# Loads of the later batches on the SP queue, and a rearranged opening of batch 0, in a cosformer attention + SwiGLU kernel

## The chip, the cores and the metric

The kernel runs on one core of a Trainium2 chip. The metric is the time of one execution in device microseconds; where several runs are given, their median. Profiles are of one execution each, recorded by the hardware.

The engines go by the profile's names: PE (TensorE, matmuls; PEld its weight loads), DVE (VectorE), ACT (ScalarE), POOL (GpSimd), SP (SyncE). Each runs its own program in order and waits at semaphores for the others. DMAs are issued by SP and ACT (hardware queues) and by POOL (software queue, which can also convert f32 to bf16 on the way).

## What is computed

A linear attention with cosine weights on 8 batches x 8 heads x 576 positions x 64, followed by an RMS norm and a SwiGLU feed-forward layer (512 to 1536 and back) on the 4608 rows that result. Inputs and output are float32.

```python
def phi(x, c, s):
    r = np.maximum(x, 0.0)
    return np.concatenate([r * c, r * s], axis=-1)   # c, s: cos and sin of pi/2 * position / 576
q_p, k_p = phi(q, cos_w, sin_w), phi(k, cos_w, sin_w)
kv = np.einsum('bhsf,bhsd->bhfd', k_p, v);  z = np.sum(k_p, axis=2)
num = np.einsum('bhsf,bhfd->bhsd', q_p, kv)
den = np.einsum('bhsf,bhf->bhs', q_p, z)[..., None] + 1e-06
x = (num / den).transpose(0, 2, 1, 3).reshape(4608, 512)
xn = x / sqrt(mean(x * x) + 1e-6) * rms_g
g = xn @ w_gate
out = (g * sigmoid(g) * (xn @ w_val)) @ w_out
```

## The kernel before

**Tiles.** Each batch has 512 main rows, as four tiles (j = 0 to 3) of 128, and 64 rest rows; the rest rows of two batches share a tile (j = 4), and the rest rows of all batches form a ninth block of the feed-forward layer. The names, in the order of the work on a batch b:

- `raw` (six buffers): q, k or v of a batch as loaded, 1 MB; `remq`, `remk`, `remv`: the rest rows. `load_piece` and `load_rest` issue the loads on the engine that they are given.
- `q_scale`: two DVE or ACT instructions make `qp`, relu(q) times cos and times sin. `qp` has to be transposed into `qpT` (one buffer): `q_tr` does it by a DMA transpose on SP; `q_tr_pe` and `q_out`, used for batches 0 and 1, by eight PE transposes and a copy.
- `k_prep`, `v_prep`: the same scaling for k (`kp`), and v as bf16 beside a column of ones (`vv`, `vvr`).
- `kvz`: 40 small matmuls (8 heads x 5 row tiles, 65 columns) sum k'v and z into PSUM; `kvz_out` copies them to `kvzs`.
- `nd`: eight matmuls of `qpT` with `kvzs` give numerator and denominator of one row tile.
- `x_of`: on DVE `den`, `rec` (reciprocal) and `xt` (product), then on ACT the sum of squares (`scr`, `ssq`) and on POOL its power -1/2 (`rs`). `xn_scale`: one DVE instruction, `xn`. `xn` must be transposed into `xnT`: by a DMA on SP (`xn_tr`), or for batches 0 to 2 on PE (`xn_tr_pe`, and `xn_out` on ACT).
- `gval`: for each of 12 column groups nn, four matmuls into `gps` (w_gate) and four into `vps` (w_val), silu on ACT (`sil`), product on DVE (`hT`). `outp`: 48 matmuls of `hT` with `wo` into `acc`; `store` copies each quarter to `osb` on ACT and SP writes it out.

**Order.** It is written by hand. The main loop goes over blocks blk = 1 to 8 and over nn = 0 to 11; a step computes `gval(blk, nn)` and a share of `outp(blk - 1)`, and beside it the attention work that two tables (`PLAN`, in which r counts steps relative to a batch) assign to the next two or three batches. What the table lists for step r is emitted ahead of the step's matmuls or behind them, and so stands at that place in every engine's program. `loads_of` emits the loads last in a step: batch 3 in halves from r = -9 on, batches 4 to 7 in quarters from r = -16 to -5, with the rest rows of an even batch and its successor behind the last piece. They go to POOL's queue, where they stand between the `rs` instructions; SP's line holds the transposes and the stores. Batches 0 to 2 and the weights are loaded in a prologue: batch 0 on SP, everything else on POOL, which first waits, in the `gate` copy, for a piece of v.

**Opening (batch 0).** q is scaled, transposed on PE, k and v prepared; then `kvz` two heads at a time, each followed by a `kvz_out` of these two heads, and `nd`, `x_of`, `xn_scale`, `xn_tr_pe` and the first two column groups by row tile (`first_steps`), before the full 512-wide groups from nn = 2 on. PSUM has eight banks: pools `gv` (gps and vps, two buffers each: four banks), `acc` (two), `att` (one tile of two banks, for `kvz` and `nd` alike).

## Time and profile before

| | us |
|---|---|
| median of 14 runs (346.6 to 354.4) | 350.13 |
| the profiled execution | 349.61 |
| span of its instructions | 347.8 |
| PE busy, share of the span | 318.3, 91% |
| DVE, ACT, POOL busy | 195.7, 152.5, 90.7 |

A page of the profile gives the busy time of each engine, the same in 40 slices, the DMA queues, the chain of work that ended last and the costliest groups of instructions. The slices show how the run is built up: the opening lies in the first four, PE is nearly full from there on, with one dent in slice 14, and the DMA engines are busy until about two thirds of the span.

```profile
PE   1459999899899499999999999999999999999993
DVE  4754687766687498579547974793574232223300
DMA  7999997386679989868988799792022100000023
q0 software_dynamic: 12144, 29.63, 33.1%
q1 hardware_dynamic: 52304, 23.60, 32.7%
```

Each digit is the busy share of a slice in tenths; the two queues, POOL's (software) and SP's (hardware), each with packets, MB and the share of 16 DMA engines' time that they took.

### The profile page before, as it was taken

Reading aid. Unit: us, or ns where it says so; the run is one execution under the profiler, and the core shown is the slowest. Engines: PE = TensorE matmul, PEld = TensorE weight load, DVE = VectorE, ACT = ScalarE, POOL = GpSimd, SP = SyncE. Lnnn points to the kernel's source line nnn. Section 1 sums busy time; section 2 is a strip of 40 time slices with the busy share of each in tenths; the row PEclk is TensorE's granted clock in tenths of the full one; section 3 lists DMA queues with packets and bytes.
Section 4 is the critical chain, followed back from the end, with each engine's and each line's share of the span. In section 5 each row is a group of like instructions: output and inputs, shape, how many; then the busy total and the mean of one; then the engine's idle time right before and its main releaser. Section 6 shows DMA issues by size and latency. Waiting matters only on the chain.

```text
span 347.8 us, 5682 instructions
## 1 busy us (share of the span) xinstructions
PE 318.3 (91%) x2096; PEld 160.5 (46%) x2096; DVE 195.7 (56%) x423; ACT 152.5 (44%) x300; POOL 90.7 (26%) x135
## 2 busy tenths in 40 slices
PE   1459999899899499999999999999999999999993
PEld 1448555455445143544454445444544444444441
DVE  4754687766687498579547974793574232223300
ACT  4625683864554146244534453444434233223221
POOL 0618641205543154049115721310010000000000
PEclk9999999999999899999999999999999999999998
DMA  7999997386679989868988799792022100000023
GB/s 245 236 234 278 308 336 210 115 223 180 222 176 189 155 201 164 226 130 174 260 135 183 177 200 138 229 227 75 32 45 62 60 30 32 30 30 33 31 63 89
DMA packets 64476, 53.59 MB, mean 154 GB/s; under 512 B 45952, under 2 KB 53632, under 8 KB 64448
## 3 DMA queue, kind: packets, MB, share of 16 engines
q0 software_dynamic: 12144, 29.63, 33.1%
q1 hardware_dynamic: 52304, 23.60, 32.7%
q8 instruction: 16, 0.26, 0.4%
q14 instruction: 12, 0.10, 0.1%
HBM read 38.01 MB, written 9.44 MB: 136 GB/s over the span
## 4 chain that ended last, share of the span: by engine, by line
PE 74%; DMA 9%; DVE 8%; ACT 4%; issue 2%; SPq 0%; POOL 0%; ACTq 0%; DVEq 0%
PE gps L341 23%; PE vps L341 23%; PE acc L378 19%; DMA qpT<-qp 4%; PE kvz L226 3%; DVE xt L273 3%; PE nd L255 3%; DMA xnT<-xn 2%; PE acc L649 1%; DVE hT L350 1%; PE tps L197 1%; DMA raw<-in_q_dram 1%; ACT scr L281 1%; DMA remv<-in_v_dram 1%; ACT sil L349 1%
## 5 line engine op out<-in xcount | busy, mean ns | idle before, releaser
L350 DVE TENSOR_TENSOR hT<-vps,sil 128x512 bf16<-128x512 f32 x108 | 74.3, 688 | 106.7 <-PE vps L341 79.8
L341 PE MATMUL gps<-xnT,wg 128*128 128x512 bf16 (+1 forms) x456 | 113.7, 373 | 0.3 <-DMA xnT<-xn 0.2
L341 PE MATMUL vps<-xnT,wv 128*128 128x512 bf16 (+1 forms) x456 | 113.4, 372 | 0.0
L378 PE MATMUL acc<-wo,hT 128*128 128x512 bf16 x384 | 97.3, 379 | 1.0 <-DVE hT L350 1.0
L349 ACT ACTIVATE sil<-gps 128x512 bf16<-128x512 f32 x108 | 63.5, 591 | 69.4 <-PE gps L341 66.9
L341 PEld LDWEIGHTS <-wv 128*128 128x128 bf16 x456 | 44.6, 100 | 50.7 <-issue 1.1
L341 PEld LDWEIGHTS <-wg 128*128 128x128 bf16 x456 | 41.9, 100 | 41.6 <-issue 1.2
L286 POOL TENSOR_TENSOR rs<-ssq,mhalf 128x1 f32<-128x1 f32 x36 | 20.3, 564 | 152.4 <-ACT scr L281 152.4
L378 PEld LDWEIGHTS <-hT 128*128 128x128 bf16 x384 | 37.5, 98 | 46.8 <-DVE hT L350 2.0
L281 ACT ACTIVATE scr<-xt 128x513 bf16<-128x513 f32 x36 | 22.9, 636 | 69.1 <-DVE xt L273 69.1
L149 ACT COPY osb<-acc 128x512 f32<-128x512 f32 x34 | 19.9, 584 | 26.3 <-PE acc L378 24.3
L294 DVE SCALAR_TENSOR_TENSOR xn<-xt,rs,gb 128x512 bf16<-128x512 f32 x36 | 26.7, 742 | 0.8 <-POOL rs L286 0.8
L273 DVE TENSOR_TENSOR xt<-nd,rec 128x512 f32<-128x512 f32 x36 | 24.9, 692 | 1.2
L255 PE MATMUL nd<-kvzs,qpT 128*128 128x65 bf16 x256 | 14.4, 201 | 8.4 <-DMA qpT<-qp 4.8
L255 PEld LDWEIGHTS <-qpT 128*128 128x128 bf16 x256 | 12.7, 103 | 16.3 <-DMA qpT<-qp 5.3
L142 DVE TENSOR_SCALAR qp<-raw,cos_tab 128x512 bf16<-128x512 f32 x32 | 16.3, 520 | 3.7 <-DMA raw<-in_q_dram 3.7
L226 PE MATMUL kvz<-vv,kp 128*128 128x65 bf16 x256 | 12.0, 199 | 4.7 <-DVE vv L151 3.6
L98 POOL DMA_DIRECT2D raw<-in_q_dram x20 | 15.2, 763 | 2.5 <-DMA raw<-in_k_dram 2.1
L98 POOL DMA_DIRECT2D raw<-in_k_dram x20 | 15.5, 779 | 1.2 <-DMA wg<-in_moe_w_gate_dram 0.8
L142 DVE TENSOR_SCALAR kp<-raw,cos_tab 128x512 bf16<-128x512 f32 x32 | 15.5, 492 | 0.0
L98 POOL DMA_DIRECT2D raw<-in_v_dram x20 | 15.4, 772 | 0.0
L226 PEld LDWEIGHTS <-kp 128*128 128x128 bf16 x320 | 11.9, 101 | 6.9 <-ACT kp L140 2.0
(65 smaller groups left out, 192.3 us busy)
## 6 DMA issues: line engine op xcount, KB each, us to landing
out_dram<-osb SPq DMA_DIRECT2D x32, 256.0 KB, 3.0
raw<-in_q_dram POOLq DMA_DIRECT2D x16, 256.0 KB, 6.5
raw<-in_k_dram POOLq DMA_DIRECT2D x16, 256.0 KB, 8.5
raw<-in_v_dram POOLq DMA_DIRECT2D x16, 256.0 KB, 3.6
raw<-in_q_dram POOLq DMA_DIRECT2D x2, 1024.0 KB, 12.6
raw<-in_k_dram POOLq DMA_DIRECT2D x2, 1024.0 KB, 13.6
raw<-in_v_dram POOLq DMA_DIRECT2D x2, 1024.0 KB, 10.5
wg<-in_moe_w_gate_dram POOLq DMA_DIRECT2D x3, 512.0 KB, 6.4
```

The lines of the kernel that those rows point to most:

```text
L98: eng.dma_start(out=raws[what, b][:, h0 : h0 + n, :], in_=src[b, h0 : h0 + n, 0:SM, :].rearrange("h (p j) d -> p h (j d)", j=NJ),)
L142: nc.vector.tensor_scalar(out=dst, in0=src, scalar1=tab[lanes, col : col + 1], scalar2=0.0, op0=ALU.mult, op1=ALU.max,)
L226: nc.tensor.matmul(kvz_ps[b][:, h // 2 % 2, c0 : c0 + DE], lhsT=kp[:, c, h, :], rhs=vv[:, c, h, :] if c < NJ else vvr[:, b % 2, h, :], sta ...
L255: nc.tensor.matmul(ps[rows, h // HH, (h % HH) * DE : (h % HH + 1) * DE], lhsT=src[:, h, cols], rhs=kz[:, h, :], start=True, stop=True,)
L273: nc.vector.tensor_tensor(out=xt[:, 0:DM].rearrange("p (g h d) -> p g h d", g=2, d=D), in0=ndv[:, :, :, 0:D], in1=rec[:, :].rearrange("p ( ...
L281: nc.scalar.activation(out=scr[:, :], in_=xt[:, :], func=AF.Square, scale=DM**-0.5, accum_out=ssq[:, :],)
L286: nc.gpsimd.tensor_tensor(out=rs[:, :], in0=ssq[:, :], in1=mhalf[:, :], op=ALU.pow)
L294: nc.vector.scalar_tensor_tensor(out=t[:, :], in0=xt[:, 0:DM], scalar=rs[:, 0:1], in1=gb[:, :], op0=ALU.mult, op1=ALU.mult,)
L341: nc.tensor.matmul(ps[:, c0 : c0 + n], lhsT=w[:, dt, nn * P : (nn + 1) * P], rhs=xnTs[blk][:, dt, c0 : c0 + n], start=(dt == 0), stop=(dt ...
L349: nc.scalar.activation(out=sil[:, :], in_=gps[:, :], func=AF.Silu)
L350: nc.vector.tensor_tensor(out=hTs[blk][:, nn, :], in0=vps[:, :], in1=sil[:, :], op=ALU.mult)
L378: nc.tensor.matmul(acc[:, :], lhsT=hTs[blk][:, nn, j * P : (j + 1) * P], rhs=wo[:, nn, :], start=(nn == 0), stop=(nn == NNT - 1),)
```

## The change

Parts:

1. `loads_of` (batches 3 to 7) issues on SP instead of POOL.
2. Every second piece of batch 0's q, and the second half of its k, are issued by ACT instead of SP.
3. POOL's `gate` waits for the second half of k instead of a piece of v; the first 512 columns of w_gate and w_val are loaded as two times 256.
4. Opening: `kvz` of batch 0 in one go into a tile of a new pool `nd` (two tiles of two banks, on the banks that `gv` takes afterwards), one `kvz_out` on DVE, and `nd` tiles in `nd` and `att`; `x_of` of three row tiles ahead of the first `xn_scale`.
5. `keep_warm`: matmuls of `ident` with a tile of zeros whose result nobody reads, at seven places of the opening.
6. `kvzs` is laid out by PSUM bank, so that `kvz_out` is one copy of 520 columns; it goes to ACT in batches 1 to 7, where before ACT and DVE each copied a half.

DVE's order in the opening, from the last casts of v on. Before:

```order
L151 CAST vv<-raw 128x4x2x64 x2
L151 CAST kvzs<-kvz 128x130 x2
L265 TENSOR_SCALAR den<-nd 128x8
L270 RECIPROCAL rec<-den 128x8
L273 TENSOR_TENSOR xt_100<-nd,rec 128x512
L265 TENSOR_SCALAR den<-nd 128x8
L270 RECIPROCAL rec<-den 128x8
L273 TENSOR_TENSOR xt_101<-nd,rec 128x512
L294 SCALAR_TENSOR_TENSOR xn<-xt_100,rs,gb 128x512
L265 TENSOR_SCALAR den<-nd 128x8
L270 RECIPROCAL rec<-den 128x8
L273 TENSOR_TENSOR xt_102<-nd,rec 128x512
```

And after the change, from the second row tile's xt on:

```order
L276 TENSOR_TENSOR xt_101<-nd,rec 128x512
L268 TENSOR_SCALAR den<-nd 128x8
L273 RECIPROCAL rec<-den 128x8
L276 TENSOR_TENSOR xt_102<-nd,rec 128x512
L297 SCALAR_TENSOR_TENSOR xn<-xt_100,rs,gb 128x512
L268 TENSOR_SCALAR den<-nd 128x8
L273 RECIPROCAL rec<-den 128x8
L276 TENSOR_TENSOR xt_103<-nd,rec 128x512
L297 SCALAR_TENSOR_TENSOR xn<-xt_101,rs,gb 128x512
L297 SCALAR_TENSOR_TENSOR xn<-xt_102,rs,gb 128x512
L297 SCALAR_TENSOR_TENSOR xn<-xt_103,rs,gb 128x512
```

The third xt has moved ahead of the first xn, and two xn now stand between the fourth xt and its own xn, where before there was one.

SP's line around batch 3's q transposes (in the program from block 1, step 2, to block 2, step 6; qpT is a transpose of q, qprT one of rest rows, xnT_108 the transposed rest rows, out_dram a store). Before:

```order
L187 DMA_TRANSPOSE qpT<-qp 128x8x128 x5
L363 DMA out_dram<-osb 128x512
L211 DMA_TRANSPOSE qprT<-qpr 128x8x128
L187 DMA_TRANSPOSE qpT<-qp 128x8x128
L309 DMA_TRANSPOSE xnT_108<-xn 128x4x128
L187 DMA_TRANSPOSE qpT<-qp 128x8x128
L363 DMA out_dram<-osb 128x512
L187 DMA_TRANSPOSE qpT<-qp 128x8x128
```

After the change, first up to the store:

```order
L188 DMA_TRANSPOSE qpT<-qp 128x8x128 x4
L99 DMA raw<-in_q_dram 128x4x256 x2
L99 DMA raw<-in_k_dram 128x4x256 x2
L99 DMA raw<-in_v_dram 128x4x256 x2
L99 DMA raw<-in_q_dram 128x2x256 x4
L111 DMA remq<-in_q_dram 64x8x64 x2
L188 DMA_TRANSPOSE qpT<-qp 128x8x128
L366 DMA out_dram<-osb 128x512
```

Then on from the store:

```order
L99 DMA raw<-in_k_dram 128x2x256
L212 DMA_TRANSPOSE qprT<-qpr 128x8x128
L188 DMA_TRANSPOSE qpT<-qp 128x8x128
L99 DMA raw<-in_k_dram 128x2x256
L312 DMA_TRANSPOSE xnT_108<-xn 128x4x128
L188 DMA_TRANSPOSE qpT<-qp 128x8x128
L366 DMA out_dram<-osb 128x512
L99 DMA raw<-in_k_dram 128x2x256
L188 DMA_TRANSPOSE qpT<-qp 128x8x128
```

All of batch 3 and the q of batch 4 (12 loads) now stand between batch 2's last transpose and batch 3's first, and one quarter of batch 4's k before each further transpose of batch 3.

The diff:

```diff
...
     iota_f = consts.tile([P, 1], FP32, name="iota_f")
     gate = consts.tile([P, 1], FP32, name="gate")
     mhalf = consts.tile([P, 1], FP32, name="mhalf")
+    zeros = consts.tile([P, SM], BF16, name="zeros")
     warm = consts.tile([P, 1], FP32, name="warm")
     raws = {}
...
     kvzs = {}
     kvz_ps = {}
-    def kvz(b, h0, n):
+    def slot_of(h):
+        return h // 2 % 2, h // HH * 2 + h % 2
+    def kvz(b, h0, n, pool="att"):
         if h0 == 0:
-            kvz_ps[b] = pools["att"].tile([P, 2, 512], FP32, name="kvz", tag="att")
-            kvzs[b] = kvz_pool.tile([P, H, DE], BF16, name="kvzs", tag="kvzs")
+            kvz_ps[b] = pools[pool].tile([P, 2, 512], FP32, name="kvz", tag=pool)
+            kvzs[b] = kvz_pool.tile([P, 2, HH, DE], BF16, name="kvzs", tag="kvzs")
         for h in range(h0, h0 + n):
-            c0 = (h // HH * 2 + h % 2) * DE
+            c0 = slot_of(h)[1] * DE
             for c in range(NJ + 1):
                 nc.tensor.matmul(
-                    kvz_ps[b][:, h // 2 % 2, c0 : c0 + DE], lhsT=kp[:, c, h, :],
+                    kvz_ps[b][:, slot_of(h)[0], c0 : c0 + DE], lhsT=kp[:, c, h, :],
                     rhs=vv[:, c, h, :] if c < NJ else vvr[:, b % 2, h, :],
                     start=(c == 0), stop=(c == NJ),
                 )
-    def kvz_out(b, bank, eng, pairs=slice(0, 2)):
-        dst = kvzs[b][:, :, :].rearrange("p (a g i) e -> p g a i e", g=2, i=2)
-        src = kvz_ps[b][:, bank, 0 : HH * DE].rearrange("p (a i e) -> p a i e", a=2, i=2)
-        copy(eng, dst[:, bank, pairs, :, :], src[:, pairs, :, :])
+    def kvz_out(b, eng):
+        src = kvz_ps[b][:, :, 0 : HH * DE].rearrange("p g (h e) -> p g h e", e=DE)
+        copy(eng, kvzs[b][:, :, :, :], src)
     nds = {}
     xts = {}
     x_count = []
     xnTs = {}
-    def nd(b, j):
-        ps = pools["att"].tile([P, 2, 512], FP32, name="nd", tag="att")
+    def nd(b, j, pool="att"):
+        ps = pools[pool].tile([P, 2, 512], FP32, name="nd", tag=pool)
         parts = (
             [(slice(0, P), qpT, slice(j * P, (j + 1) * P), kvzs[b])]
             if j < NJ
...
             for h in range(H):
                 nc.tensor.matmul(
                     ps[rows, h // HH, (h % HH) * DE : (h % HH + 1) * DE],
-                    lhsT=src[:, h, cols], rhs=kz[:, h, :], start=True, stop=True,
+                    lhsT=src[:, h, cols], rhs=kz[:, slot_of(h)[0], slot_of(h)[1], :], start=True, stop=True,
                 )
         nds[b, j] = ps
...
     for e in range(4):
-        load_piece("q", q, 0, 2 * e, 2, nc.sync)
+        load_piece("q", q, 0, 2 * e, 2, nc.scalar if e % 2 else nc.sync)
     for e in range(2):
-        load_piece("k", k, 0, HH * e, HH, nc.sync)
+        load_piece("k", k, 0, HH * e, HH, nc.scalar if e % 2 else nc.sync)
     for what, src in (("k", k), ("v", v)):
         load_rest(what, src, 0, nc.sync)
     for e in range(4):
...
     )
     nc.gpsimd.iota(iota_i[:, :], pattern=[[0, 1]], base=0, channel_multiplier=1)
     masks.make_identity(nc, ident[:, :])
-    nc.gpsimd.tensor_copy(out=gate[:, :], in_=raws["v", 0][:, 2, 0:1])
-    load_wgv(0)
+    nc.gpsimd.tensor_copy(out=gate[:, :], in_=raws["k", 0][:, HH, 0:1])
+    load_wgv(0, 256)
+    load_wgv(256, 256)
     load_wgv(512)
     load_first("q", 1)
     load_first("k", 1)
+    nc.vector.memset(zeros[:, :], 0.0)
     nc.vector.memset(warm[:, :], 0.0)
     nc.vector.memset(mhalf[:, :], -0.5)
     for t in xt_ring:
...
-    for name, bufs in (("gv", 2), ("acc", 2), ("att", 1)):
-        pools[name] = ctx.enter_context(
-            tc.tile_pool(name="ps" + name, bufs=bufs, space=bass.MemoryType.PSUM)
-        )
+    def open_psum(name, bufs):
+        return tc.tile_pool(name="ps" + name, bufs=bufs, space=bass.MemoryType.PSUM)
     V, A = nc.vector, nc.scalar
-    q_scale(0, 0, V, A)
-    q_scale(0, 1, V, A)
-    q_scale(0, 2, V, A)
-    q_tr_pe(0, 0)
-    q_out(0, 0, V)
-    q_scale(0, 3, V, A)
-    for j, eng in ((1, A), (2, V), (3, A)):
-        q_tr_pe(0, j)
-        q_out(0, j, eng)
-    for c in range(NJ):
-        k_prep(0, c, V, A if c < 3 else V)
-    k_prep(0, NJ, V, V)
-    v_prep(0, NJ, V)
-    for e in range(4):
-        v_prep_heads(0, 2 * e, 2, A if e % 2 else V)
-    for e in range(4):
-        kvz(0, 2 * e, 2)
-        kvz_out(0, e % 2, V if e % 2 else A, slice(e // 2, e // 2 + 1))
+    for name, bufs in (("acc", 2), ("att", 1)):
+        pools[name] = ctx.enter_context(open_psum(name, bufs))
+    def keep_warm(n, pool="fill"):
+        ps = pools[pool].tile([P, SM], FP32, name="fill", tag=pool)
+        for _ in range(n):
+            nc.tensor.matmul(ps[:, :], lhsT=ident[:, :], rhs=zeros[:, :], start=True, stop=True)
+    with open_psum("fill", 1) as pools["fill"]:
+        keep_warm(12)
+        q_scale(0, 0, V, A)
+        q_scale(0, 1, V, A)
+        q_scale(0, 2, V, A)
+        q_tr_pe(0, 0)
+        q_out(0, 0, V)
+        q_scale(0, 3, V, A)
+        for j, eng in ((1, A), (2, V), (3, A)):
+            keep_warm(2)
+            q_tr_pe(0, j)
+            q_out(0, j, eng)
+        keep_warm(8)
+        for c in range(NJ):
+            k_prep(0, c, V, A if c < 3 else V)
+        k_prep(0, NJ, V, V)
+        v_prep(0, NJ, V)
+        for e in range(4):
+            v_prep_heads(0, 2 * e, 2, A if e % 2 else V)
+    with open_psum("nd", 2) as pools["nd"]:
+        kvz(0, 0, H, "nd")
+        kvz_out(0, V)
+        keep_warm(2, "acc")
+        nd(0, 0, "nd")
+        nd(0, 1)
+        nd(0, 2, "nd")
+        x_of(0, 0)
+        x_of(0, 1)
+        nd(0, 3)
+        x_of(0, 2)
+        keep_warm(8, "acc")
+    pools["gv"] = ctx.enter_context(open_psum("gv", 2))
     def first_steps(j):
         for nn in range(2):
             gval_mm(0, nn, j * P, P)
-    nd(0, 0)
-    x_of(0, 0)
-    nd(0, 1)
-    x_of(0, 1)
-    nd(0, 2)
     xn_scale(0, 0)
-    x_of(0, 2)
     xn_tr_pe(0, 0)
     xn_out(0, 0)
-    nd(0, 3)
+    x_of(0, 3)
     xn_scale(0, 1)
+    first_steps(0)
     xn_tr_pe(0, 1)
     xn_out(0, 1)
-    first_steps(0)
-    x_of(0, 3)
-    xn_scale(0, 2)
-    xn_tr_pe(0, 2)
-    xn_out(0, 2)
-    first_steps(1)
-    xn_scale(0, 3)
-    xn_tr_pe(0, 3)
-    xn_out(0, 3)
-    first_steps(2)
+    for j in (2, 3):
+        xn_scale(0, j)
+        xn_tr_pe(0, j)
+        xn_out(0, j)
+        first_steps(j - 1)
     first_steps(3)
     gval_end(0, 0)
     gval_end(0, 1)
...
         i, e = divmod(r - first, cut)
         what, src = (("q", q), ("k", k), ("v", v))[i]
         n = H // cut
-        load_piece(what, src, b, n * e, n, nc.gpsimd)
+        load_piece(what, src, b, n * e, n, nc.sync)
         if e == cut - 1 and b % 2 == 0:
-            load_rest(what, src, b, nc.gpsimd)
-            load_rest(what, src, b + 1, nc.gpsimd)
+            load_rest(what, src, b, nc.sync)
+            load_rest(what, src, b + 1, nc.sync)
     def plan_of(**whats):
         plan = {}
...
             elif what == "v":
                 v_prep(b, n, V if b == 2 and n % 2 else A)
             elif what == "kvz_out":
-                kvz_out(b, 0, A)
-                kvz_out(b, 1, V)
+                kvz_out(b, A)
             elif what == "xn_out":
                 xn_out(b, n)
             elif what == "x":
...
         accs[0, j] = pools["gv"].tile([P, DM], FP32, name="acc", tag="gv"[j % 2])
     for nn in range(NNT):
         if nn == 0:
-            kvz_out(1, 0, A)
-            kvz_out(1, 1, V)
+            kvz_out(1, A)
         if nn in (1, 3, 5, 7):
             x_of(1, nn // 2)
         if nn in (4, 6, 8, 10):
```

## The prediction

> **What bounds the kernel now.** I read the page first, then busy time by stretches, then what TensorE (PE) waits for, then the timeline of the two stretches that lose time.
>
> ```profile
> span 347.8 us, 5682 instructions
> PE 318.3 (91%) x2096; PEld 160.5 (46%) x2096; DVE 195.7 (56%) x423; ACT 152.5 (44%) x300; POOL 90.7 (26%) x135
> ```
>
> PE is busy 91% of the span, so a gain can only come from its idle time, or from time in which it is busy but slow. The stretches show where those are (start:end, length, busy time of PE, PEld, VectorE (DVE), ScalarE (ACT), GpSimd (POOL), granted clock, DMA share, GB/s).
>
> ```profile
> 0.00:32.70 32.70, 16.50 (x185) 14.46 (x186) 17.21 (x62) 15.68 (x31) 12.86 (x24) 1.00 0.99 251
> 32.70:114.80 82.10, 79.92 (x595) 40.80 (x594) 59.16 (x123) 48.35 (x95) 31.55 (x44) 1.00 0.83 215
> 114.80:123.10 8.30, 3.48 (x16) 1.57 (x17) 3.27 (x8) 1.93 (x6) 2.04 (x4) 0.79 1.03 153
> 123.10:137.30 14.20, 13.57 (x82) 6.17 (x81) 13.62 (x30) 7.65 (x16) 8.09 (x12) 1.00 1.07 175
> 137.30:331.40 194.10, 193.73 (x1170) 92.68 (x1171) 101.74 (x202) 75.94 (x150) 36.14 (x53) 1.00 0.52 117
> 331.40:347.80 16.40, 11.06 (x52) 4.80 (x49) 0.69 (x1) 2.93 (x5) 0.00 (x0) 0.90 0.32 80
> ```
>
> From 137.3 to 331.4 PE misses 0.4 us of 194: nothing can be won there, only lost. The tail after 331.4 isn't touched. What is left is the opening, with 16.2 us of idle PE, and one hole at 114.8, with 4.8 us of it and a granted clock of 0.79. The list of what PE waits for names the same places.
>
> ```profile
> PE nd L255 <- DMA qpT<-qp: 4.8, 1, 4.8
> ...
> PE nd L255 <- DVE xt L273: 3.4, 5, 1.2
> ```
>
> **The opening, step by step.** Its timeline, with the rows that carry the steps (start, length, engine, line, operation; in brackets the idle time before it and what ended it):
>
> ```profile
> 0.74 2.00 SPq L98 DMA_DIRECT2D raw<-in_q_dram  x4
> 6.97 1.28 DVE L142 TENSOR_SCALAR qp<-raw,cos_tab 128x512 bf16<-128x512 f32 x3 [3.68 <-DMA raw<-in_q_dram]
> 11.99 0.18 POOL L400 COPY gate<-raw 128x1 f32<-128x1 f32 x1 [10.51 <-DMA raw<-in_v_dram]
> 15.29 0.38 PE L226 MATMUL kvz<-vv,kp 128*128 128x65 bf16 x4 [3.56 <-DVE vv L151]
> ...
> 19.40 0.29 DVE L151 CAST kvzs<-kvz 128x130 bf16<-128x130 f32 x1 [1.93 <-PE kvz L226]
> 19.75 0.60 PE L255 MATMUL nd<-kvzs,qpT 128*128 128x65 bf16 x8 [0.45 <-DVE kvzs L151]
> 20.38 0.17 DVE L265 TENSOR_SCALAR den<-nd 128x8 f32<-128x8 f32 x1 [0.69 <-PE nd L255]
> 20.82 0.69 DVE L273 TENSOR_TENSOR xt<-nd,rec 128x512 f32<-128x512 f32 x1
> ...
> 26.36 0.69 DVE L273 TENSOR_TENSOR xt<-nd,rec 128x512 f32<-128x512 f32 x1
> 28.53 0.75 DVE L294 SCALAR_TENSOR_TENSOR xn<-xt,rs,gb 128x512 bf16<-128x512 f32 x1 [0.82 <-POOL rs L286]
> ...
> 29.48 0.63 PE L341 MATMUL gps<-xnT,wg 128*128 128x128 bf16 x4
> ...
> 31.16 0.39 PE L341 MATMUL gps<-xnT,wg 128*128 128x128 bf16 x4
> ...
> 31.61 0.39 PE L341 MATMUL gps<-xnT,wg 128*128 128x128 bf16 x4
> ...
> 32.68 1.02 PE L341 MATMUL gps<-xnT,wg 128*128 128x512 bf16 x4
> ```
>
> The same four matmuls take 0.63 us at 29.48 and 0.39 us at 31.16: before about 30 us PE runs at a slower pace, though the clock column says 1.00 (the rows decide). Two rows from later give the prices of a warm PE and of a wider copy:
>
> ```profile
> 51.89 1.25 PE kvz L226 x40
> ```
>
> ```profile
> 108.00 0.43 DVE L151 CAST kvzs<-kvz 128x260 bf16<-128x260 f32 x1
> ```
>
> *Loads to kvz (6.97 to 15.29).* Four q issues on SP take 2.00 us, 0.5 each; with every second one on ACT's queue the last leaves 1 us earlier. The transfers themselves aren't shortened, so I take half of it, 0.5 us. [...] Bounds: 1 us lost to 1.3 us won. Term: **-0.5**.
>
> *kvz to the first nd (15.29 to 19.75, 4.46 us).* Four rounds of ten matmuls, each waiting for a copy of the round before out of the one PSUM tile, become 40 matmuls and one copy. At the warm price that is 1.25; the copy costs 0.43 for 260 columns and 0.29 for 130, so about 0.14 for 130 more and 0.71 for 520; 0.35 goes for the two hand-overs. 2.3 instead of 4.46: **-2.15**. With PE at its slow pace (four rounds of about 0.7, 2.8 in all) it would be -0.6.
>
> *The x chain (20.38 to 29.28, 8.9 us).* nd now has three tiles in flight, so DVE never waits for PE: den, rec, xt take 1.13 us (20.38 to 21.51). In the new order (see the rows of DVE in the change) the fourth xt ends after four of these and one xn of 0.7, at 5.2 us, where before it was at 26.36 + 0.69 - 20.38 = 6.7. The last xn then starts 1.48 us after it, as before (27.05 to 28.53: ACT's square, POOL's power), because the two xn between them take as long. 5.2 + 1.5 + 0.75 = 7.45: **-1.45**; another -0.15 because a warm nd gives its first result sooner (0.63 from 19.75 to 20.38 before).
>
> *Last xn to the first full group (29.28 to 32.68, 3.4 us).* PE was behind by then at its slow pace. Warm, what remains is a transpose, two first_steps of 0.9 each (two pairs of gps and vps, 0.45 from 31.16 to 31.61) and 0.4 for the rest, 2.2: **-1.2**.
>
> The dummy matmuls (12, 2, 2, 2, 8, 2, 8 of them) fill time in which PE waits anyway: at 0.22 us each warm, the longest batch is 1.7 us, and the last of these lies beside 4 us of DVE work. They cost nothing if PE arrives before its inputs; if one is late by a whole batch, 1.7.
>
> Opening: **-5.4**; with each term at its bound -1.2 to -6.7 (the best of the x chain leaves out the 0.3 that POOL's power is now awaited). What could take it back is the weights, since PE then asks for everything 5.4 us sooner:
>
> ```profile
> 44.63 0.78 POOL L131 DMA_DIRECT2D wo<-in_moe_w_out_dram  x1 [0.77 <-DMA wo<-in_moe_w_out_dram]
> ```
>
> ```profile
> DMA to landing us min/median/max: 11.3/11.3/11.3
> ```
>
> ```profile
> 61.17 1.89 PE L649 MATMUL acc<-wo,hT 128*128 128x512 bf16 x8
> ```
>
> This last third of wo lands at 55.9; its first use is the second half of the row at 61.17, at 62.0, or 56.6 after the change. The queue ahead of it starts earlier, too: the gate row waited until 11.99 for a piece of v, and k's second half is issued four issues of 0.5 to 1 us ahead of that piece. So it just holds; if the queue doesn't start earlier, up to 1 us is lost, which stays inside the bounds.
>
> **The hole at 114.8.**
>
> ```profile
> 119.62 0.62 PE L255 MATMUL nd<-kvzs,qpT 128*128 128x65 bf16 x8 [4.85 <-DMA qpT<-qp]
> 120.05 1.90 PE L341 MATMUL gps<-xnT,wg 128*128 128x512 bf16 x4
> 121.73 1.56 PE L341 MATMUL vps<-xnT,wv 128*128 128x512 bf16 x4
> ...
> 124.04 1.02 PE L341 MATMUL gps<-xnT,wg 128*128 128x512 bf16 x4
> ```
>
> PE waits 4.85 us for the third transpose of batch 3's q, and then runs two groups slowly: 1.90 - 1.02 and 1.56 - 1.02 are 1.4 us more. Together 6.3. Why the transpose was late, from the chain, from SP's and from POOL's timeline:
>
> ```profile
> 105.70 13.87 DMA qpT<-qp
> ```
>
> ```profile
> 73.45 23.49 SPq L187 DMA_TRANSPOSE qpT<-qp  x5
> ...
> 105.70 3.73 SPq L187 DMA_TRANSPOSE qpT<-qp  x1
> ```
>
> ```profile
> 102.07 2.19 POOL L98 DMA_DIRECT2D raw<-in_k_dram  x3
> ```
>
> Issued 9 us ahead of its use, it took 13.87 us to land, and SP itself was held 3.73 us, while three k quarters and what follows on POOL's queue ran on the same DMA engines: the stretch 114.8 to 123.1 has them at 1.03 busy with only 153 GB/s. After the change those loads stand in SP's line, one between two transposes (see SP's rows). By the order, batch 3 and the q of batch 4 go out in one burst of 12 loads behind batch 2's four transposes and ahead of batch 3's first. Of the five transposes from 73.45 on these are four and one: the four end by about 79, the fifth at 96.94, 18 us apart; 4.3 MB at the 251 GB/s of the opening are 17 us, so the burst is just over when the fifth is due. From there the third transpose has two transposes, one xnT and two quarter loads of 256 KB (1 us each) ahead of it: it lands some 5 us after issue instead of 14.
>
> Not all 6.3 come back, because **DVE is late next**: in 114.8 to 137.3 it works 3.27 + 13.62 = 16.9 of 22.5 us, so no more than 5.6 can go, and I leave it 0.4 of small waits. Term: **-5.2**, bounds 0 to -6.3.
>
> SP's own time: 12 loads and three remainders more in a block are about 8 us of issue in 32 us (194.1 / 6), beside ten transposes of 1.3 and five stores. It fits. The loads wait for no busy buffer: each reuses a tile whose readers finished over ten steps before. The one wider kvzs copy on ACT in blocks 1 to 7 hides behind the 2 us between kvz and nd: nothing.
>
> **Sum.** The profiled execution took 349.61, its span 347.8 and 1.8 around it. -5.4 - 5.2 gives 339.0; the median of the 14 runs, 350.13, lies 0.5 higher, so I predict 339.5.
>
> **The rivals.**
>
> *The transposes stay late.* For it: the engines are the same 16, and they were full. Against it: they moved only 153 GB/s then, so the mix, not the sum, was slow. Only the opening counts: 344.7. [...]
>
> *PE stays slow in the opening,* because DVE-bound gaps of up to 2 us lie between the dummy batches. Then kvz gives -0.6 and the first_steps give nothing: -2.7 instead of -5.4, 342.2. For it: the group at 29.48 is still slow, although by then PE has worked with short breaks for ten us. [...]
>
> *Slower: SP's line becomes the bound.* Each transpose now waits for the loads before it, in every block.
>
> ```profile
> L309 SPq DMA_TRANSPOSE xnT<-xn x1: 1191/1191/1191, 159.2 to 159.2; - x1
> ...
> DMA to landing us min/median/max: 7.7/7.7/7.7
> ```
>
> ```profile
> 170.63 1.03 PE L341 MATMUL gps<-xnT,wg 128*128 128x512 bf16 x4
> ```
>
> The last xnT that block 4 needs at 170.6 lands at 166.9: 3.7 us to spare. If it lands more than that later, PE stalls, and pays 1.4 more for the slow groups behind it. In the five blocks 4 to 8, stalls of 0.7 + 1.4 already eat the gain, so it decides at landings of about 12 us; the 13.87 above shows that such exist. With 1.5 us stalls: 339.5 + 5 x 2.9 = 354. Against it: those long landings are with two queues competing.
>
> **Chances.** Forecast 0.60, transposes stay late 0.18, PE stays slow 0.14, SP bound 0.08. The forecast's own range is 337 to 342 (both terms at their best give 337.1); taking in the first two rivals and 0.5 of scatter, 336.5 to 346. The SP rival is left out with its 0.08. A measurement of this kernel tells about 0.5% (1.8 us) from no change: faster 0.92, within 0.03, slower 0.05.
>
> **What would show it.** In the new profile: kvz at about 14.8 with no copy inside its 40 matmuls, the first nd near 17, the first 512-wide group near 27; 128-wide groups of four at 0.39 us from the start; no wait of nd for qpT; qpT landing under 8 us; DVE nearly without a break where the hole was, and perhaps a wait of PE for hT at the end of block 2. Wrong would be: a first 512-wide group after 30, nd or gps waiting for a transpose in any block from 3 on, or weights that end a wait between 27 and 60.

## The result, and the profile after

The changed kernel takes 339.17 us (median of 10 runs, 337.95 to 341.39) against 349.63 us for the kernel before on the same chips (median of 47 runs, 346.60 to 354.40 but for one of 565.93): a ratio of 0.9717, 95% interval [0.9693, 0.9742], or 2.8% less time. The execution that was profiled took 338.81 us. Its page, with the slices of PE and the two queues that the change shifts bytes between:

```profile
PE 320.5 (95%) x2132; PEld 158.4 (47%) x2132; DVE 190.5 (57%) x416; ACT 152.9 (45%) x298; POOL 42.5 (13%) x71
...
PE   7669999999899999999999999999999999999994
...
q1 hardware_dynamic: 73792, 39.86, 46.0%
q0 software_dynamic: 7920, 12.32, 14.7%
```

The dent in slice 14 is gone, the opening is fuller (part of that is dummy work: PE's busy time rose by 2.2 us), and 16 to 17 MB have moved from q0 to q1. The busy time by stretches (columns as in the prediction; the cuts are the first full group, the first group of block 3, and the same 194.1 us from there as before):

```profile
0.00:28.50 28.50, 20.78 (x220) 12.99 (x221) 17.56 (x62) 14.70 (x29) 14.00 (x26) 0.94 1.08 276
28.50:127.20 98.70, 95.09 (x693) 48.01 (x693) 72.94 (x156) 58.30 (x115) 18.61 (x28) 1.00 0.83 219
127.20:321.30 194.10, 193.69 (x1172) 92.56 (x1171) 99.29 (x199) 76.95 (x150) 9.91 (x18) 1.00 0.47 118
```

The opening is 4.2 us shorter (32.7 to 28.5), the stretch from there to block 3 is 5.9 us shorter (before 82.1 + 8.3 + 14.2 = 104.6), the long stretch is as full as it was (193.69 of 194.10), and the tail behind it gives the last 0.7 (16.4 to 15.7). In the list of what PE waits for, no wait of nd for qpT is left. In its place stand the waits that come next: nd for xt, and the output matmuls for hT. Both are seen in PE's timeline of block 2:

```profile
110.18 0.41 PE L258 MATMUL nd<-kvzs,qpT 128*128 128x65 bf16 x8
...
116.10 0.57 PE L258 MATMUL nd<-kvzs,qprT 128*64 128x65 bf16 x16 [0.52 <-DVE xt L276]
...
126.96 0.39 PE L381 MATMUL acc<-wo,hT 128*128 128x512 bf16 x1 [0.90 <-DVE hT L353]
```

The third nd, at 110.18, starts without a bracket: its transpose was there. 0.52 and 0.90 us are handed back to DVE. The two q transposes issued between 100 and 110 us landed this many us after their issue:

```profile
DMA to landing us min/median/max: 2.8/3.4/3.9
```

### The profile page after: what moved, and what is told of

Read it like the earlier page. It is cut to its first block, busy times and chain, and to the rows that moved or that the text cites. A ratio compares the mean times of both kernels' runs of the same rounds, so it can differ in the third digit from the quotient of the medians.

```text
span 337.0 us, 5731 instructions
## 1 busy us (share of the span) xinstructions
PE 320.5 (95%) x2132; PEld 158.4 (47%) x2132; DVE 190.5 (57%) x416; ACT 152.9 (45%) x298; POOL 42.5 (13%) x71
## 3 DMA queue, kind: packets, MB, share of 16 engines
q1 hardware_dynamic: 73792, 39.86, 46.0%
q0 software_dynamic: 7920, 12.32, 14.7%
q10 hardware_dynamic: 1072, 1.05, 0.9%
## 4 chain that ended last, share of the span: by engine, by line
PE 80%; DVE 12%; ACT 4%; issue 3%; DVEq 0%; ACTq 0%
PE gps L344 24%; PE vps L344 24%; PE acc L381 21%; DVE hT L353 3%; PE kvz L230 3%; DVE xt L276 3%; PE fill L463 3%; DVE xn L297 2%; PE nd L258 2%; PE acc L664 2%; ACT sil L352 1%; ACT scr L284 1%; PE tps L198 1%; DVE rec L273 1%; DVE qp L143 1%
## 5 line engine op out<-in xcount | busy, mean ns | idle before, releaser
L344 PE MATMUL gps<-xnT,wg 128*128 128x512 bf16 (+1 forms) x456 | 111.9, 368 | 1.2 <-ACT xnT L150 1.1
L344 PE MATMUL vps<-xnT,wv 128*128 128x512 bf16 (+1 forms) x456 | 111.9, 368 | 0.0
L381 PE MATMUL acc<-wo,hT 128*128 128x512 bf16 x384 | 97.3, 379 | 1.5 <-DVE hT L353 1.5
L297 DVE SCALAR_TENSOR_TENSOR xn<-xt,rs,gb 128x512 bf16<-128x512 f32 x36 | 26.7, 743 | 2.0 <-POOL rs L289 2.0
L150 ACT CAST vv<-raw 128x512 bf16<-128x512 f32 x26 | 14.8, 620 | 4.0 <-DMA raw<-in_v_dram 4.0
L143 DVE TENSOR_SCALAR qp<-raw,cos_tab 128x512 bf16<-128x512 f32 x32 | 15.0, 478 | 2.4 <-DMA raw<-in_q_dram 2.4
L258 PEld LDWEIGHTS <-qpT 128*128 128x128 bf16 x256 | 11.5, 97 | 9.8 <-issue 2.4
L143 DVE TENSOR_SCALAR kp<-raw,cos_tab 128x512 bf16<-128x512 f32 x32 | 15.3, 485 | 0.0
L258 PE MATMUL nd<-kvzs,qpT 128*128 128x65 bf16 x256 | 12.9, 193 | 2.2 <-DVE xt L276 1.8
L463 PE MATMUL fill<-zeros,ident 128*128 128x512 bf16 x36 | 12.0, 481 | 2.3 <-DVE warm L411 2.3
L230 PE MATMUL kvz<-vv,kp 128*128 128x65 bf16 x256 | 10.8, 193 | 2.2 <-ACT vv L150 2.2
L230 PEld LDWEIGHTS <-kp 128*128 128x128 bf16 x320 | 10.7, 97 | 4.3 <-ACT vv L150 2.7
L664 PE MATMUL acc<-wo,hT 128*128 128x512 bf16 x48 | 11.5, 379 | 0.0
```

What stands on the lines that cost most here:

```text
L143: nc.vector.tensor_scalar(out=dst, in0=src, scalar1=tab[lanes, col : col + 1], scalar2=0.0, op0=ALU.mult, op1=ALU.max,)
L150: nc.scalar.copy(out=dst, in_=src)
L230: nc.tensor.matmul(kvz_ps[b][:, slot_of(h)[0], c0 : c0 + DE], lhsT=kp[:, c, h, :], rhs=vv[:, c, h, :] if c < NJ else vvr[:, b % 2, h, :], ...
L258: nc.tensor.matmul(ps[rows, h // HH, (h % HH) * DE : (h % HH + 1) * DE], lhsT=src[:, h, cols], rhs=kz[:, slot_of(h)[0], slot_of(h)[1], :], ...
L297: nc.vector.scalar_tensor_tensor(out=t[:, :], in0=xt[:, 0:DM], scalar=rs[:, 0:1], in1=gb[:, :], op0=ALU.mult, op1=ALU.mult,)
L344: nc.tensor.matmul(ps[:, c0 : c0 + n], lhsT=w[:, dt, nn * P : (nn + 1) * P], rhs=xnTs[blk][:, dt, c0 : c0 + n], start=(dt == 0), stop=(dt ...
```

## The experiments

The kernels compute all of the reference. "Block 2" is the time from ACT's first silu of block 2 to the first of block 3, "full group" the start of the first 512-wide group; both come from the profiled execution, the medians from all runs. Each ratio is to the kernel before as it ran beside that kernel, so ratios compare better than medians from different rows; two rows whose intervals overlap are not told apart.

| kernel | median us (range) | ratio to before, 95% | full group | block 2 |
|---|---|---|---|---|
| before | 349.63 (346.60 to 354.40, one 565.93) | 1 | 32.68 | 40.78 |
| the change | 339.17 (337.95 to 341.39) | 0.9717 [0.9693, 0.9742] | 28.51 | 35.06 |
| queue alone | 343.38 (342.68 to 343.75) | 0.9823 [0.9769, 0.9877] | 31.93 | 35.08 |
| opening alone | 344.53 (341.94 to 345.35) | 0.9839 [0.9780, 0.9899] | 27.28 | 41.95 |
| last 8 dummies removed | 340.06 (339.01 to 340.62) | 0.9721 [0.9673, 0.9768] | 29.67 | 35.07 |
| dummies moved | 337.87 (337.56 to 339.17) | 0.9669 [0.9621, 0.9717] | 27.23 | 35.06 |
| loads on ACT | 339.94 (338.39 to 340.67) | 0.9735 [0.9695, 0.9775] | 28.67 | 35.95 |
| no dummies | 340.08 (339.64 to 340.89) | 0.9741 [0.9703, 0.9778] | 30.60 | 35.06 |
| batch 0 on one queue | 340.09 (339.85 to 340.64) | 0.9747 [0.9715, 0.9779] | 29.40 | 35.05 |
| the change again | 339.15 (337.90 to 339.47) | 0.9696 [0.9669, 0.9723] | 27.31 | 35.07 |
| dummies moved, again | 337.88 (337.09 to 339.20) | 0.9668 [0.9640, 0.9697] | 27.74 | 35.07 |
| loads on ACT, bunched | 345.00 (343.53 to 347.00) | 0.9871 [0.9802, 0.9940] | 27.55 | 40.08 |
| loads on POOL, paced | 338.78 (338.30 to 339.66) | 0.9677 [0.9634, 0.9721] | 27.09 | 36.11 |
| dummies moved, 8 more | 337.89 (337.24 to 340.04) | 0.9645 [0.9619, 0.9670] | 29.75 | 35.07 |

### The two halves apart

The queue alone, in the kernel before (and the same lines back to `nc.gpsimd` in the changed kernel, for the opening alone):

```diff
-        load_piece(what, src, b, n * e, n, nc.gpsimd)
+        load_piece(what, src, b, n * e, n, nc.sync)
...
-            load_rest(what, src, b, nc.gpsimd)
-            load_rest(what, src, b + 1, nc.gpsimd)
+            load_rest(what, src, b, nc.sync)
+            load_rest(what, src, b + 1, nc.sync)
```

> The kernel before, with only the loads of batches 3 to 7 moved to SP's line. Theory (the transposes were late because loads on the second, software queue competed with them): the wait of nd for qpT at 114.8 (4.85 us) and the 1.4 us of slow groups behind it go, a wait for hT of about 1 us comes at the end of block 2, qpT lands under 5 us; block 3 starts 5.7 us earlier, 349.6 - 5.7 = 344. Rival (the hole went because the opening moved everything): the wait stays at 4 to 5 us, time 349 to 350.

> The changed kernel with the loads of batches 3 to 7 back on POOL's queue. Theory: the opening keeps its 4.2 to 4.4 us (first 512-wide group at 28.5, block 2 at 92.1), and a wait of nd for qpT of 4 to 5 us is there again in block 2, with a qpT that takes over 10 us to land: 349.6 - 4.4 = 345.2. Rival (the hole depends on the timing of the opening): no such wait, 339 to 340.

Both came out within a us of the forecast: 343.38 and 344.53. Against the 349.08 of the kernel before in the runs beside them the queue gives 5.7 and the opening 4.55 us, 10.25 together, and the whole change gave 10.5 (the ratios multiply to 0.967, measured 0.9717, which the two intervals allow): no sign that one half depends on the other. With the queue alone PE has no wait for qpT, and the three q transposes issued between 100 and 112 us land in 2.9 to 4.6 us. With the opening alone the hole is there as before. PE's row, and the landing of the two q transposes issued between 100 and 110 us in that run:

```profile
114.94 0.62 PE L258 MATMUL nd<-kvzs,qpT 128*128 128x65 bf16 x8 [5.41 <-DMA qpT<-qp]
```

```profile
DMA to landing us min/median/max: 11.3/13.1/14.8
```

Block 2 takes 40.78 and 41.95 us with the loads on POOL and 35.08 and 35.06 with them on SP, behind the old and the new opening. The queue alone keeps the two half copies of `kvzs`, so the one wide copy of part 6 gives nothing in block 2. The parts of the opening (3 and 4) were not tried one by one; their shares are read from the steps of the profile further down.

### Why the transposes were late: which queue, or how many loads at once

With the loads on POOL the same run shows what stood beside the late transposes (SP's and POOL's timeline):

```profile
95.79 0.69 POOL L289 TENSOR_TENSOR rs<-ssq,mhalf 128x1 f32<-128x1 f32 x1 [4.76 <-ACT scr L284]
96.43 2.19 POOL L99 DMA_DIRECT2D raw<-in_k_dram  x3
98.61 1.62 POOL L111 DMA_DIRECT2D remk<-in_k_dram  x2
...
100.06 4.92 SPq L188 DMA_TRANSPOSE qpT<-qp  x1
100.23 0.70 POOL L99 DMA_DIRECT2D raw<-in_v_dram  x1
...
106.12 4.81 SPq L188 DMA_TRANSPOSE qpT<-qp  x1
```

POOL had waited for ACT's square until 95.79 (its `rs`), and then issued six loads in 4.5 us: three of k, two rests of k, and at 100.23 one of v (six, where two of the expectations below speak of eight). So the change did two things: it put the loads on another queue, and it spaced them, since on SP they stand between transposes that wait for their inputs. Three kernels take these apart. First, ACT's hardware queue (q10 on that run's page, where SP's is q1), which isn't in line with the transposes but is paced by ACT's work in each step (`nc.sync` becomes `nc.scalar` in the three lines above):

> The changed kernel, with the loads from batch 3 on issued by ScalarE (a hardware queue of their own, one or two loads per step of the block) in place of SP. Theory 'software queue, issued in bunches': the transposes were late because GpSimd, held by its own waits, issued eight loads within 4.5 us beside them through the software queue; ScalarE issues its loads one per step, so the time from the first silu of block 2 to that of block 3 stays near 35.1 us, transposes land in under 6 us, and the run takes 338.5 to 341 us (72 issues lie in ScalarE's idle time). Rival 'only one line helps': the transposes are late whenever loads go through any other queue, because only the order within one queue keeps loads away from them; then block 2 takes 40 to 42 us and the run 344 to 346 us.

339.94 us and 35.95 for block 2: the rival falls, the loads needn't be in the transposes' line. One number of the theory was off, a landing of 7.0 us where under 6 was expected. PE did not wait for it, as the transposes are issued some 9 us ahead of their use (at 101.31 and 103.99, for nd at 110.68 and 113.76). Then the two ways to separate the queue from the spacing: six loads on ACT's queue issued one behind the other, and POOL's software queue held to the pace of the steps.

```diff
-                if b < B:
+                if b < B and not (b == 4 and -11 <= r <= -8):
                     loads_of(b, r)
+                if b == 4 and r == -10:
+                    for late in range(-11, -7):
+                        loads_of(b, late)
```

> As the run with ScalarE's queue, but six of batch 4's loads (three pieces of k, both rests of k, the first piece of v) are issued one behind the other in the third step of block 2, about as GpSimd did beside the late transposes. Theory 'bunch': so many loads at once beside the transposes make them late, whatever the queue; then transposes land 10 us or more after their issue there, block 2 takes 38 to 42 us and the run 342 to 346 us. Rival 'software queue': its loads alone make the transposes late, one hardware queue beside another does not; then the landings stay under 8 us, block 2 at 35.9 to 36.5 us, and the run at 339.5 to 340.5 us.

```diff
-    def loads_of(b, r):
+    def loads_of(b, r, pace):
...
-        load_piece(what, src, b, n * e, n, nc.sync)
+        nc.gpsimd.tensor_copy(out=gate[:, :], in_=pace)
+        load_piece(what, src, b, n * e, n, nc.gpsimd)
...
-                    loads_of(b, r)
+                    loads_of(b, r, hTs[blk][:, nn, 0:1])
```

> The changed kernel, with the loads from batch 3 on issued by GpSimd through the software queue again, but each held back by a small copy (128x1, into a tile that nothing reads) that reads the hT of the step in which it is issued, so that the loads go out one or two per step and not eight in 4.5 us. Theory 'bunch': then the transposes land within 7 us, block 2 takes 35 to 36.5 us and the run 338.8 to 340.5 us. Rival 'software queue': a transpose beside a load of that queue is late also when there is only one; then landings of 8 us and more stay, block 2 takes 38 us or more and the run 342 to 346 us.

The bunch on ACT cost 5 us, as its theory had it, but not by its mechanism. The three q transposes issued between 97 and 110 us landed in

```profile
DMA to landing us min/median/max: 4.4/4.5/5.0
```

so they weren't late. What was late is ACT itself. Its issues (ACTq) and its silu, and below them the same two rests where ACT issues one or two loads per step:

```profile
102.01 3.94 ACTq L111 DMA_DIRECT2D remk<-in_k_dram  x2
...
107.06 0.60 ACT L352 ACTIVATE sil<-gps 128x512 bf16<-128x512 f32 x1 [6.67 <-DMA qpT<-qp]
...
108.20 0.41 PE L258 MATMUL nd<-kvzs,qpT 128*128 128x65 bf16 x8 [3.55 <-ACT kvzs L150]
```

```profile
103.28 1.31 ACTq L111 DMA_DIRECT2D remk<-in_k_dram  x2
```

Two rest loads took 3.94 us to issue, where 1.31 was enough when the loads came step by step. The silu stands behind these issues in ACT's program and started when they were done: ACT had computed nothing for 6.67 us (the bracket names a transpose, but the last issue, of 0.37 us at 106.59, ends just ahead of the silu), and PE waited 3.55 us for the kvzs copy behind it. The issues themselves were stretched and so lay apart; it isn't a clean bunch on the DMA engines, and whether one would have made the transposes late on a hardware queue stays open.

The paced software queue is the clear one: 338.78 us, no slower than the change, with the loads on the queue that was suspected. Its timeline at the place, and the landings of the two q transposes of 101.02 and 103.00:

```profile
101.02 1.26 SPq L188 DMA_TRANSPOSE qpT<-qp  x1
...
101.65 0.73 POOL L99 DMA_DIRECT2D raw<-in_k_dram  x1 [0.16 <-issue]
...
103.00 1.49 SPq L188 DMA_TRANSPOSE qpT<-qp  x1
103.04 0.73 POOL L99 DMA_DIRECT2D raw<-in_k_dram  x1 [0.28 <-issue]
103.77 1.38 POOL L111 DMA_DIRECT2D remk<-in_k_dram  x2
...
105.27 0.71 POOL L99 DMA_DIRECT2D raw<-in_v_dram  x1
...
113.91 0.42 PE L258 MATMUL nd<-kvzs,qpT 128*128 128x65 bf16 x8 [2.06 <-DMA qpT<-qp]
```

```profile
DMA to landing us min/median/max: 3.9/7.4/10.9
```

The transpose with one load in the 2 us behind its issue landed in 3.9 us, the one with four in the 2.3 us behind it in 10.9, and only for that one in the whole run did PE wait, 2.06 us; block 2 took 1.05 us longer than in the change (36.11 against 35.06). Both theories had a number wrong: landings within 7 us didn't hold, and block 2 didn't take 38. What the runs show is that spacing the loads on the software queue takes nearly all of the loss away. It doesn't take the rests of k for it: in the kernel before, a transpose issued at 130.44 us, with three q loads issued from 129.90 on and three of k from 132.09 on, landed in 10.0 us. How many loads make a transpose late isn't settled: in the paced run one issued at 184.60 us, with three loads in the 2.3 us behind it, landed in 2.8.

### The opening: dummy matmuls and PE's pace

In the profile of the changed kernel the opening gained less than its steps had promised. PE, DVE, ACT and POOL from the first nd on:

```profile
16.10 0.91 PE L258 MATMUL nd<-kvzs,qpT 128*128 128x65 bf16 x24 [0.36 <-DVE kvzs L152]
...
18.77 0.42 PE L258 MATMUL nd<-kvzs,qpT 128*128 128x65 bf16 x8 [1.76 <-DVE xt L276]
19.03 3.36 PE L463 MATMUL fill<-zeros,ident 128*128 128x512 bf16 x8
22.18 0.63 PE L318 MATMUL tpx<-ident,xn 128*128 128x128 bf16 x4
22.85 0.59 ACT L150 COPY xnT<-tpx 128x512 bf16<-128x512 bf16 x1 [2.29 <-PE tpx L318]
23.33 0.64 ACT L284 ACTIVATE scr<-xt 128x513 bf16<-128x513 f32 x1
24.13 0.55 POOL L289 TENSOR_TENSOR rs<-ssq,mhalf 128x1 f32<-128x1 f32 x1 [2.94 <-ACT scr L284]
24.72 0.75 DVE L297 SCALAR_TENSOR_TENSOR xn<-xt,rs,gb 128x512 bf16<-128x512 f32 x1 [1.95 <-POOL rs L289]
```

Read it from the end: the last xn waits 1.95 us for POOL, POOL for ACT's fourth square, which stands behind the first xnT copy in ACT's line; that copy waits for the first tpx, and tpx for eight dummy matmuls that take 3.36 us, 0.43 each, although its xn was ready at 20.40 (19.66 + 0.74). The clock granted to PE shows the same: 0.50 from 19.4 to 22.7 us, where a second profile of the same kernel (shown below) has 1.00 throughout (columns as in the stretches; the clock is the third number from the end):

```profile
19.40:22.70 3.30, 3.30 (x12) 1.38 (x10) 3.23 (x7) 0.85 (x4) 1.10 (x2) 0.50 1.24 206
19.40:22.70 3.30, 2.57 (x27) 1.56 (x26) 3.19 (x8) 2.38 (x7) 1.24 (x3) 1.00 1.25 206
```

The half pace follows a gap of 1.76 us; the eight nd right behind the gap still run at full pace (0.42 us, 0.62 when slow). Two kernels, one without the last eight dummies, one with eight of them moved into that gap and four left behind it:

```diff
         nd(0, 2, "nd")
+        keep_warm(8, "acc")
         x_of(0, 0)
...
-        keep_warm(8, "acc")
+        keep_warm(4, "acc")
```

> The changed kernel without its last eight dummy matmuls. In the changed kernel these take 3.36 us (0.43 each) because PE had gone slow in the 1.76 us gap before them, and the first transpose of xn starts at 22.18, 1.8 us after its xn. Theory: without them that transpose starts at about 20.5 and the last xn ends near 24.0 instead of 25.5, but PE does the 128-wide groups at the slow pace (0.63 us for four instead of 0.39), so the first 512-wide group comes at 27.5 to 28.8 and the time is 338.3 to 339.5. Rival (the dummy matmuls keep nothing fast): the 128-wide groups stay at 0.39, first 512-wide group at 26.8, 337.4.

> The changed kernel with eight dummy matmuls between the third and the fourth nd of the opening, where PE idles for 1.76 us, and four instead of eight behind the fourth nd. Theory (the gap makes PE slow): all twelve take 0.22 us each, the first transpose of xn starts at 20.4 instead of 22.2, the last xn ends near 23.8, first 512-wide group at 26.7 instead of 28.5, time 337.4. Rival (PE is slow there for the low share of work before, not for this gap): they take 0.43 each, the fourth nd comes 1.7 us later than before, the first 512-wide group at 28.5 to 30, time 339 to 341.

Without the last eight, the gap of 1.76 is followed by one of 1.27, and PE's groups are slow far into the first column groups:

```profile
19.55 0.42 PE L258 MATMUL nd<-kvzs,qpT 128*128 128x65 bf16 x8 [1.76 <-DVE xt L276]
21.25 0.61 PE L318 MATMUL tpx<-ident,xn 128*128 128x128 bf16 x4 [1.27 <-DVE xn L297]
...
22.91 0.63 PE L344 MATMUL vps<-xnT,wv 128*128 128x128 bf16 x4
```

340.06 us: worse than either theory had it (up to 339.5). In its profile kvz, too, started 0.78 us later than in the first profile of the change (14.72 against 13.94). By the medians the eight are worth 0.9 us, but the ratios, 0.9721 and 0.9717, don't tell the two kernels apart. With the gap filled the groups take 0.39 us from the first on:

```profile
17.73 1.67 PE L463 MATMUL fill<-zeros,ident 128*128 128x512 bf16 x7
...
22.42 0.39 PE L344 MATMUL vps<-xnT,wv 128*128 128x128 bf16 x4
```

The full group then starts at 27.23, and the run takes 337.87 us (26.7 and 337.4 were expected, but kvz started 0.67 us later than in the profile that these come from). But the opening alone, whose program is that of the changed kernel up to batch 3's loads, had shown its eight dummies at full pace behind the same gap. So both were run again, side by side:

> The changed kernel once more, beside the version with four of its dummy matmuls moved. In two profiled executions with the same opening the eight dummy matmuls behind the fourth nd took 3.36 us (the changed kernel's own) and about 1.9 us (the one with GpSimd's loads), behind the same gap of 1.76 us. Theory: that gap leaves TensorE's pace open, execution by execution, so the profile shows the first full group either at about 27.3 or at about 28.5 us and the median stays at 338.7 to 339.5 us. Rival: the pace is settled by the code, and the other profile differed for its own reasons; then the first full group is at 28.5 again.

> The changed kernel with eight dummy matmuls in the gap ahead of the fourth nd and four behind it, once more, on the same chip as the changed kernel. Theory: no gap over 0.7 us is left for TensorE between nd and the first full group, so its pace holds in every execution: first full group at 27.2, run 0.8 to 1.5 us under the changed kernel's median of the same call (337.7 to 338.2 us). Rival: the difference of 1.3 us between the first two runs was scatter; then the two medians lie within 0.4 us.

The changed kernel's second profile (one of the eight records is missing in it):

```profile
19.23 0.42 PE L258 MATMUL nd<-kvzs,qpT 128*128 128x65 bf16 x8 [1.76 <-DVE xt L276]
...
19.71 1.67 PE L463 MATMUL fill<-zeros,ident 128*128 128x512 bf16 x7
...
23.67 0.75 DVE L297 SCALAR_TENSOR_TENSOR xn<-xt,rs,gb 128x512 bf16<-128x512 f32 x1 [0.44 <-POOL rs L289]
```

The same program, the same gap, and this time no loss: full group at 27.31, last xn without the 1.95 us. Seven profiled executions have this gap (1.60 to 1.76 us) and the eight dummies behind it. One lost its pace there, the changed kernel's own first profile. Four kept it throughout (the second profile, the opening alone, the bunched loads on ACT, the paced ones). The other two, loads on ACT and batch 0 on one queue, lost it earlier, in kvz behind waits of 3.10 and 2.19 us, and had it back before this gap; their full groups come at 28.67 and 29.40. In the changed kernel's first profile the clock stood at 0.50 for 3.4 us (19.29 to 22.70). In the other two the slow rows last about as long: from 15.14 to some 18.5 and from 15.39 to some 18.8, ends estimated from the 24 nd that take 1.26 and 1.03 us there, 0.91 at full pace and 1.48 in the run without dummies. The theory for the moved dummies, that the pace holds in every execution, failed in its own second profile: it was lost in kvz, behind a wait of 2.80 us, and the full group came at 27.74, no sooner than the changed kernel's 27.31. The medians differ by 1.27 us in these two kernels' second runs and 1.30 between the first ones, as expected, but the intervals of the ratios, [0.9640, 0.9697] and [0.9669, 0.9723], overlap a little. That the moved dummies help is likely; that they do so by saving the pace at this gap isn't shown.

Without any dummies at all (all seven batches taken out):

> The changed kernel without any of its dummy matmuls. Theory: they keep TensorE at its full pace in the kvz and nd steps and behind them, so without them kvz takes 1.0 us longer, the three nd 0.5 us, and the 128-wide groups go at 0.63 instead of 0.39 us until about 28 us as in the run without the last eight; first full group 1.5 to 3 us later than in the profile of the changed kernel (28.51), run 340.5 to 342.2 us. Rival: TensorE's pace is off the path there, since each step waits for VectorE or ScalarE; then no more than the run without the last eight, 340.1 us, within 0.3.

The median, 340.08 us, is the rival's number, but the profile is the theory's: kvz to the first nd takes 3.15 instead of 2.16 us, the 128-wide groups 0.63, and the full group comes at 30.60, so PE's pace is on the path there. The profiled execution, 340.89 us, was the longest of four, and four runs don't settle which of the two is the rule. All dummies together are worth 0.9 us by the medians, which the intervals of the ratios don't tell from nothing (0.9741 [0.9703, 0.9778] without, 0.9717 and 0.9696 with). Moved, they are clear of no dummies at all: 0.9668 [0.9640, 0.9697], 2.2 us by the medians. The last idea, eight more dummies in the wait of PE ahead of kvz, on top of the moved ones:

```diff
-        keep_warm(8)
+        keep_warm(16)
         for c in range(NJ):
             k_prep(0, c, V, A if c < 3 else V)
```

> The version with moved dummy matmuls, with 16 instead of 8 of them between the transposes of q and kvz, where TensorE waits 2.2 to 3.1 us for v. In three profiled executions kvz or the two dummies behind it ran slowly (the two dummies 1.04 instead of 0.60 us) after such a gap. Theory: eight more (1.8 us) leave a gap of 0.4 to 1.3 us, kvz keeps its pace in every execution, and the run takes 337.2 to 337.7 us, up to 0.6 us less than with eight. Rival: what kvz loses there is waited for by nobody, or the pace was lost in few executions only; then 337.7 to 338.2 us as before. If the dummies held kvz up, it would start after 15.0 us and the run take 338.5 us or more.

337.89 us against 337.88, with ratios of 0.9645 and 0.9668 whose intervals overlap: no gain is shown, and one of the size that was expected, up to 0.6 us, isn't ruled out. Its profile can't say more, since it fell on the longest of the seven executions (340.04), in which DVE worked slowly between 10 and 17 us (four kp in 2.57 us, 1.92 in the changed kernel's second profile) and kvz started at 16.68; the other six took 337.24 to 338.05. Why DVE was slow there wasn't found.

### The second load queue

```diff
-        load_piece("q", q, 0, 2 * e, 2, nc.scalar if e % 2 else nc.sync)
+        load_piece("q", q, 0, 2 * e, 2, nc.sync)
...
-        load_piece("k", k, 0, HH * e, HH, nc.scalar if e % 2 else nc.sync)
+        load_piece("k", k, 0, HH * e, HH, nc.sync)
```

> The changed kernel, with batch 0's q and k pieces all on SP again. Theory: the second queue is what brought the last q piece forward by 1.14 us (6.85 to 5.71) and kvz by 1.35 us; with one queue kvz starts 1.0 to 1.4 us later (15.0 to 15.3 in place of 13.94), run 340.2 to 340.6 us. Rival: kvz waits for the last v piece, which the bytes ahead of it decide (13.34 before, 12.90 after), so that kvz starts at most 0.5 us later and the run takes 339.2 to 339.7 us.

```profile
7.38 1.28 DVE L143 TENSOR_SCALAR qp<-raw,cos_tab 128x512 bf16<-128x512 f32 x3 [3.81 <-DMA raw<-in_q_dram]
...
15.39 0.37 PE L230 MATMUL kvz<-vv,kp 128*128 128x65 bf16 x4 [2.19 <-DVE vv L152]
```

340.09 us and kvz at 15.39, near the theory's 340.2 and 15.3 and beyond the rival's ranges. The other profiles bear it out: kvz starts at 13.94 to 14.84 us in the ten with two queues (14.47 on average, without the one in which DVE was slow) and at 15.22 to 15.39 in the three with one (the kernel before and the queue alone are the others). So the second queue brings kvz forward by 0.4 to 1.5 us, 0.8 on average. That q's landing does it alone isn't shown: from the first qp to kvz are 7.99 to 8.89 us in these profiles. Nor are the 0.9 us of the median all of this origin for certain: in this profile PE also lost its pace in kvz (3.15 us to the first nd instead of 2.16), and the intervals of the ratios overlap.

## Why the prediction was right, step by step

Forecast 339.5 us, measured 339.17; for the profiled execution 339.0 and 338.81. The opening, in us, with the steps of the prediction, in the first and the second profile of the changed kernel:

| step | forecast | first profile | second profile |
|---|---|---|---|
| loads to kvz | -0.5 | -1.35 | -0.89 |
| kvz to the first nd | -2.15 | -2.30 | -2.30 |
| first nd to den | -0.15 | -0.18 | -0.18 |
| x chain, den to the end of the last xn | -1.45 | +0.02 | -1.49 |
| last xn to the first full group | -1.2 | -0.36 | -0.51 |
| opening | -5.4 | -4.17 | -5.37 |

- **Loads to kvz** was sized too small. "The transfers themselves aren't shortened, so I take half of it" is the term that was off: over all profiles the second queue brings kvz forward by 0.8 us on average (0.4 to 1.5), most of the 1 us of issue time and not half. The average stays inside the term's bounds, of which the 1 us lost was the author's estimate that no run shows.
- **kvz to the first nd** was right where PE keeps its pace: one sweep of 40 matmuls and one copy, 2.16 us where 2.3 was reckoned. Where it lost it in kvz, this took 2.61 to 3.15.
- **The x chain** was right where PE keeps its pace (7.41 us, forecast 7.45) and worth nothing where it doesn't. The close agreement is partly luck: in the second profile the fourth xt ends 4.90 us after the first den starts, not 5.2, and the last xn starts 1.76 us behind it, not 1.5, because it waits 0.44 for POOL. The sentence on the dummies, "they cost nothing if PE arrives before its inputs; if one is late by a whole batch, 1.7", named the risk: in the first profile the last batch was late, and tpx started 1.78 us after its xn was ready.
- **Last xn to the first full group** was sized too large in every profile. PE is at its full pace, yet it isn't idle when the last xn comes at 24.42 (second profile): the first steps of the row tile ahead still run, so 2.9 us remain and not 2.2.
- **The hole** gave 5.72 us (block 2, 40.78 to 35.06) where 5.2 was forecast, of 6.3 that could go. The third transpose landed in 2.8 us where some 5 were reckoned, and the next wait is the one named, DVE: in 110 to 122 us it works 11.10 of 12, and PE waits 0.52 for xt and 0.90 for hT at the end of block 2. The reason given, "those loads stand in SP's line, one between two transposes", holds for the place of the loads; that they changed queue was not needed, as the paced run shows.

```profile
110.00:122.00 12.00, 11.43 (x80) 5.40 (x79) 11.10 (x26) 6.76 (x16) 2.27 (x4) 1.00 0.77 187
```

The total came nearer than its terms, and that is luck: in the first profile the opening gave 1.2 us less and the rest 1.4 more (the hole 0.5, the tail 0.7, which no step had, and 0.2 in block 1). In the second the opening gave what was forecast and the rest 1.1 more, and that execution took 337.90 us.

**The rivals.** *The transposes stay late* (344.7) is what the opening alone shows, 344.53, so its price was right and its premise wrong. SP, ACT and a paced POOL came within 1.2 us of one another (339.17, 339.94 and 338.78), so the choice of the queue alone decided little; the move took the wait of nd for qpT away because it also set when the loads are issued. *PE stays slow in the opening* never came about for the whole of it, but in three profiles of seven PE was slow for about 3.4 us; in the changed kernel's own this cost 1.2 us (full group at 28.51 against 27.31). That PE keeps its pace over gaps of up to 2 us, as the forecast took it, was the author's estimate, and it did not hold each time: behind 1.76 us of idling the clock went to 0.50 in the changed kernel's first profile and stayed at 1.00 in its second. *SP's line becomes the bound* did not happen: from block 3 on PE is busy 193.69 of 194.10 us.

The versions with the dummies moved are the fastest that were run: 337.87 to 337.89 us, ratios of 0.9645 to 0.9669.
